# An FFN unit list in block order with a table of cluster limits, in a fused attention and maxout-FFN kernel

## The chip, the cores and the metric

The kernel runs on one NeuronCore of a Trainium2 chip. The metric is the device time of one execution in microseconds, lower being better. A core has five engines that run beside each other and wait for each other by semaphores: TensorE (PE; its weight loads are listed apart as PEld), VectorE (DVE), ScalarE (ACT), GpSimd (POOL) and SyncE (SP, which here only issues DMAs). Matmul results go to PSUM, which this kernel uses as eight banks of 128 x 512 fp32.

## What is computed

Attention over B = 8 batches, H = 8 heads, S = 576 tokens and D = 64, with 16 extra "beacon" keys and values that every query sees, and then a maxout FFN on all 4608 tokens:

```python
k_all = np.concatenate([beacon_k, k], axis=2)
v_all = np.concatenate([beacon_v, v], axis=2)
scores = scale * np.matmul(q, k_all.transpose(0, 1, 3, 2))
scores = np.where(causal, -1000000000.0, scores)
a = softmax(scores)
x = np.matmul(a, v_all).transpose(0, 2, 1, 3).reshape(B * S, H * D)
h = np.maximum(np.maximum(x @ w1, x @ w2), x @ w3)      # 512 -> 768
out = h @ w_out                                         # 768 -> 512
```

## The kernel before

**Attention in pairs.** Two heads make a pair p, four pairs (pi = 0 to 3) a batch b, and there are 32 pairs. From pair 8 on each pair is one turn of the loop at line 1027. `emit_burst` (line 526) issues its scores as 12 small matmuls (L517) into all eight PSUM banks, and ScalarE takes the exponentials (L534) four times, a pair of banks each. `emit_masks` (L556) has GpSimd clear what lies behind the diagonal. At an even p, `emit_pv_whole` (line 614) multiplies the two pairs before it with the values (L634, 108 and more matmuls into four banks), and ScalarE copies the result out (L644, L645) and makes the reciprocal of the sums (L650 to L652). What remains, the product of both, is `finish` (L657): two VectorE multiplies of 128 x 576, one for each 128 rows of `xT`, the FFN's transposed input. `finish` is issued only after the FFN units of that turn. At pi = 0 it writes the last values of the batch before, and so raises `ready`.

**FFN in units.** The 4608 tokens are nine blocks tb of 512. A block has 18 mm1 units (three weight matrices times six slices of 128 hidden features; four matmuls L709 that accumulate over the four row groups ct of `xT`, and one VectorE operation that starts the maximum (L726) or joins it (L728) in the tile `hT`) and four mm2 units (128 tokens each; six matmuls L756 with `hT` as weights, one VectorE copy L763 into a tile `y`, and a store on SP, L788). Block 0 counts twelve half units and six whole ones in place of the 18. So there are 22 units a block (UPB) and 198 in all. Blocks of 512 tokens do not fall together with batches of 576: nearly all blocks need the last values of a batch. Each unit carries in `need` the value of `ready` from which it may be issued.

**The order of the work** is written out by hand and nothing reorders it. The list `units` (lines 793 to 811) gives the sequence of the units. In it, a block tb from 1 on begins with its own first two mm1 units, then come the four mm2 units of block tb - 1, then its other 16 mm1 units. (Block 0's mm2 units stand behind its own mm1 units.) In each turn of the pair loop the cluster of units that follows the scores goes on until `allowed` (lines 1033 to 1037), which grows evenly by 22 units for four pairs, or until a unit's `need` is not met. The last unit of a cluster is issued with `close`, which cuts it into two halves of 256 columns (`parts`, L717), so that the last PSUM eviction before the next burst is short. Inside the cluster, the transposes of the next pair come after the first unit (only for p + 1 < 16), and `plan`'s entries for (p, 0) after the second: casts on GpSimd (L267, L310), loads (L229, L294), stores of cast pairs to DRAM (L379) and their transposing fetches (L386, L387) on SP. `store_y` issues a store of every `y` that was complete before the present unit.

PSUM banks are handed out in turn (`next_bank`, L156); a burst takes the pairs of banks that have been free longest (`next_pairs`, L161).

After the last pair (lines 1059 to 1068), three units are issued, then the last `emit_pv_whole`, then two units, then `finish`, and then all units that are left.

Of the kernel before, what the change touches and what calls it, by code (L numbers as in the profile page):

```python
# [16 lines left out]
def kernel(  # L17
# [23 lines left out]
    TOKB = 512  # L41
# [18 lines left out]
    PPB = H // 2  # L60
# [23 lines left out]
    FIRST_BURST = 2 * PPB  # L84
# [350 lines left out]
    def place_beacons(p, copy):  # L435
        b, pi = divmod(p, PPB)
        copy(kTs[p % NT][:, 0:Nb], bT[:, pi, Nb * b : Nb * (b + 1)])
# [54 lines left out]
    def emit_scores(p, gi):  # L492
        if gi == 0:
            at[p] = at_pool.tile([128, AT_W], BF16, name="at_sb")
        kT = kTs[p % NT]
        qT = qTs[p % NT]
        ps = sc_psum.tile()
        off = 0
        for t, q0, q1 in groups(p)[gi]:
            for e in range(2):  # L500
                hs = slice(64 * e, 64 * e + 64)
                nc.tensor.matmul(  # L502
                    ps[:, e, off : off + q1 - q0],
                    kT[hs, 128 * t : 128 * t + 128],
                    qT[hs, q0:q1],
                    start=True,
                    stop=True,
                    tile_position=(64 * e, 0),
                )
            off += q1 - q0  # L510
        nc.scalar.activation(  # L511
            out=both_heads(p, gi), in_=ps[:, :, 0 : g_width(p, gi)], func=AF.Exp, scale=scale
        )
# [29 lines left out]
    def emit_masks(p, gi, dve=False):  # L543
        masked.add((p, gi))
        off = 0
        for t, q0, q1 in groups(p)[gi]:
            n = rows_of(p, t, q1)
            lo, hi = max(q0, k_tok[t]), min(q1, k_tok[t] + n)
            if lo < hi:
                view = both_heads(p, gi)[0:n, :, off + lo - q0 : off + hi - q0]  # L550
                x0 = lo - k_tok[t]
                if dve:
                    m = tri[0:n, None, x0 : x0 + hi - lo]
                    nc.vector.tensor_mul(view, view, m.to_broadcast([n, 2, hi - lo]))
                else:
                    nc.gpsimd.affine_select(  # L556
                        out=view,
                        in_=view,
                        compare_op=ALU.is_ge,
                        fill=0.0,  # L560
                        base=x0,
                        pattern=[[0, 2], [1, hi - lo]],
                        channel_multiplier=-1,
                    )
            off += q1 - q0
# [225 lines left out]


    units = []
    outputs = []
    for tb in range(n_tokb):
        need = 2 * ((TOKB * (tb + 1) - 1) // S) + 1
        blocks = []
        if tb == 0:
            for n, lo in ((0, 0), (need, MID)):
                for i in range(2):  # L800
                    for ft in range(0, n_ft, 2):
                        units.append((n, mm1_halves, (tb, ft, i, lo, lo + MID)))
        for i in range(2 if tb == 0 else 0, 3):
            for ft in range(n_ft):
                blocks.append((need, mm1_unit, (tb, ft, i)))
        units += blocks[:2] + outputs + blocks[2:]
        outputs = [(need, mm2_unit, (tb, tt)) for tt in range(TOKB // 128)]
        if tb == 0:
            units += outputs
            outputs = []  # L810
    units += outputs
    END = len(units)
    UPB = END // n_tokb
    done = [0]
# [48 lines left out]
    def start():  # L863
        keep_busy(12)
        load_half(0, 0, nc.sync)
        load_half(0, 1, nc.scalar)
        load_half(1, 0, nc.sync)
        load_beacons(0, 1, bk32_0, nc.scalar)
        load_half(1, 1, nc.scalar)
        make_identity(nc, ident)  # L870
        nc.gpsimd.memset(tri, 1.0)
        nc.gpsimd.affine_select(
            out=tri,
            in_=tri,
            compare_op=ALU.is_ge,
            fill=0.0,
            base=0,
            pattern=[[1, 128]],
            channel_multiplier=-1,
        )  # L880
        load_quad(1, 0)
        load_quad(0, 1)
        load_quad(1, 1)
        next_load(3)
        cast_half(0, 0, by_dve)
        cast_half(0, 1, by_act)
        by_dve(bk16_0, bk32_0)
        turn_half(0, 0, False, by_act)
        keep_busy(3)
        turn_beacons(0, 1, bk16_0)  # L890
        cast_half(1, 0, by_dve)
        cast_half(1, 1, by_dve)
        keep_busy(2)
        turn_half(1, 0, True)
        place_beacons(1, by_dve)
# [6 lines left out]
    def steps(p):  # L902
        return [[0, 1], [2, 3]]
# [55 lines left out]
    for b in range(2, B):  # L959
        p = b * PPB  # L960
# [5 lines left out]
    for b in range(B_PE, B):  # L966
        p = b * PPB
# [7 lines left out]
    N_FIRST = 11  # L975

    def emit_all():
        start()
        for group, fns in first_steps:
            if group:  # L980
                emit_scores(*group)
            for fn in fns:
                fn()
        first = done[0]
        n_step = 0
        n_y = 0
        for p in range(PPB, FIRST_BURST):
            for s, gs in enumerate(steps(p)):
                for gi in gs:
                    emit_scores(p, gi)  # L990
                for gi in gs:
                    emit_masks(p, gi)
                for args in pv_at.pop((p, s), ()):
                    emit_pv(*args)
                    invert_sums()

                n_step += 1
                allowed = first + n_step * (UPB - first) / N_FIRST
                if s == 0:
                    if p == PPB + 2:  # L1000
                        emit_ffn(allowed)
                    turn_pair(p + 1, by_act, "pv" if p < PPB + 2 else "sc")
                    if p != PPB + 2:
                        emit_ffn(allowed)
                    place_beacons(p + 1, by_act)
                    store_y(n_y)
                    n_y = len(y_out)
                    for fn in plan.pop((p, s), ()):
                        fn()
                    emit_ffn(allowed)  # L1010
                    n_y = len(y_out)
                    emit_ffn(allowed)
                    multiply()
                else:
                    emit_ffn(allowed)
                    multiply()
                    store_y(n_y)
                    n_y = len(y_out)
                    for fn in plan.pop((p, s), ()):
                        fn()  # L1020
                    emit_ffn(allowed)
                    n_y = len(y_out)
                while emit_ffn(allowed):
                    pass
        v_tiles.pop(0)

        for p in range(FIRST_BURST, NPAIR):
            b, pi = divmod(p, PPB)
            emit_burst(p)
            finish = emit_pv_whole(p // 2 - 1) if p % 2 == 0 else None  # L1030
            for gi in range(NG):
                emit_masks(p, gi)
            n_step += 2
            if n_step <= N_FIRST:
                allowed = first + n_step * (UPB - first) / N_FIRST
            else:
                allowed = UPB + (n_step - N_FIRST) * UPB / (2 * PPB)
            n = 0
            while may_emit(allowed):
                n_y = len(y_out)  # L1040
                emit_ffn(allowed, next_psum, not may_emit(allowed, 1))
                store_y(n_y)
                n += 1
                if n == 1 and p + 1 < B_PE * PPB:
                    turn_pair(p + 1, by_act, "any")
                    place_beacons(p + 1, by_act)
                if n == 2:
                    for fn in plan.pop((p, 0), ()):
                        fn()
            assert n >= 2  # L1050
            if finish:
                finish()
            for s in range(2):
                for fn in plan.pop((p, s), ()):
                    fn()
            if pi == 0:
                v_tiles.pop(b - 1)
        assert not plan and not loads and not pv_at
        for _ in range(3):
            emit_ffn(END, next_psum)  # L1060
        finish = emit_pv_whole(NPAIR // 2 - 1)
        for _ in range(2):
            emit_ffn(END, next_psum)
        finish()
        store_y(len(y_out))
        while emit_ffn(END - 1, next_psum):
            store_y(len(y_out))
        mm2_last(n_tokb - 1, TOKB // 128 - 1, (0, 320, 512))
# [33 lines left out]
```

## Time and profile before

| | us |
|---|---|
| median of three runs | 300.87 (299.56 to 300.94) |
| the profiled execution | 301.9 |
| its span, first to last instruction | 300.2 |
| PE busy | 282.3 (94%) |
| DVE, ACT, POOL busy | 180.9, 148.0, 132.7 |
| mean granted TensorE clock | 0.983 |

A profile is of one execution. Its page gives each engine's busy time, the span in 40 slices of 7.5 us, the chain of waits that ended last, and groups of instructions by source line; line numbers such as L709 are those of the kernel before. In a timeline, a row has the start in us, the time from the start of its first instruction to the end of its last, the engine, the line, the operation, the count, and in brackets the engine's idle time before it with what ended it. Matmuls overlap each other in the pipeline, so the distance between their starts, not their own duration, says how fast they go.

### The profile page before, as it was taken

What the parts mean: (1) busy time and instruction counts of PE and PEld (TensorE: products, weight loads), DVE (VectorE), ACT (ScalarE), POOL (GpSimd) and SP (SyncE); (2) the same over time, 40 slices, a digit from 0 to 9 for tenths busy, and PEclk for the clock granted to TensorE, in tenths of its full rate; (3) what the DMA queues carried; (4) which work ended last, traced back from release to release, by engine and by line L of the source; (5) the groups of instructions that cost most, each with busy time, mean ns of one, the idle gap of its engine ahead of it and who ended that gap; (6) DMA issues with size and microseconds to landing.
All of it is one profiled execution on the core that took longest, in us unless ns stands there. A gap on an engine that the chain in (4) does not pass through costs nothing.

```text
span 300.2 us, 8579 instructions
## 1 busy us (share of the span) xinstructions
PE 282.3 (94%) x3511; PEld 163.2 (54%) x3539; DVE 180.9 (60%) x330; ACT 148.0 (49%) x247; POOL 132.7 (44%) x253
## 2 busy tenths in 40 slices
PE   7789997999999999999999999999999998999994
PEld 3545664465656465546555787465546453444442
DVE  3743763537585649473847384738473856776772
ACT  3664485796667484747474747474746430000000
POOL 6170667476566864566456635663262300000000
PEclk9966999999999999999999999999999999999999
DMA  8978999999999999799979996997303000202103
GB/s 149 199 126 197 232 203 271 260 198 285 270 216 249 171 306 229 164 175 289 290 154 181 276 265 161 196 257 130 82 11 131 2 2 35 105 3 84 56 0 142
DMA packets 85319, 50.66 MB, mean 169 GB/s; under 512 B 64416, under 2 KB 80032, under 8 KB 85280
## 3 DMA queue, kind: packets, MB, share of 16 engines
q1 hardware_dynamic: 80672, 45.76, 66.0%
q0 software_dynamic: 4048, 4.03, 8.2%
q8 instruction: 27, 0.44, 0.7%
q10 hardware_dynamic: 560, 0.33, 0.5%
q14 instruction: 12, 0.10, 0.1%
HBM read 35.13 MB, written 14.22 MB: 164 GB/s over the span
## 4 chain that ended last, share of the span: by engine, by line
PE 78%; DMA 9%; DVE 5%; issue 2%; POOL 2%; SPq 1%; ACT 1%; POOLq 0%
PE acc L709 41%; PE acc L756 15%; PE acc L634 10%; DMA st<-in_v_dram 8%; PE acc L517 6%; DVE xT L657 3%; PE acc L600 2%; DVE hT L728 2%; PE acc L394 2%; ACT at_sb L511 1%; PE acc L502 1%; DMA h<-in_q_dram 1%; SPq L229 1%; POOL v_sb L310 1%; PE acc L737 1%
## 5 line engine op out<-in xcount | busy, mean ns | idle before, releaser
L709 PE MATMUL acc<-xT,w_sb 128*128 128x512 bf16 (+1 forms) x709 | 135.5, 340 | 4.5 <-DVE xT L657 3.3
L534 ACT ACTIVATE at_sb<-acc 128x416 bf16<-128x416 f32 (+1 forms) x96 | 75.3, 868 | 69.3 <-PE acc L517 58.5
L709 PEld LDWEIGHTS <-w_sb 128*128 128x128 bf16 x732 | 69.1, 98 | 59.8 <-issue 4.4
L556 POOL TENSOR_SCALAR_AFFINE_SELECT at_sb<-at_sb 128x256 bf16<-128x256 bf16 (+2 forms) x148 | 58.7, 411 | 89.9 <-ACT at_sb L534 71.6
L728 DVE TENSOR_TENSOR hT<-hT,acc 128x512 bf16<-128x512 bf16 (+1 forms) x119 | 69.8, 610 | 37.3 <-PE acc L709 34.7
L726 DVE CAST hT<-acc 128x512 bf16<-128x512 f32 (+1 forms) x49 | 33.1, 680 | 31.0 <-PE acc L709 23.0
L756 PE MATMUL acc<-w_out_sb,hT 128*128 128x512 bf16 (+1 forms) x241 | 46.8, 347 | 0.2
L267 POOL CAST p<-st 96x768 bf16<-96x768 f32 x56 | 44.5, 825 | 0.0
L763 DVE COPY y<-acc 128x512 f32<-128x512 f32 (+1 forms) x41 | 24.7, 613 | 18.8 <-PE acc L756 17.7
L756 PEld LDWEIGHTS <-hT 128*128 128x128 bf16 x246 | 23.9, 98 | 21.8 <-DVE hT L728 0.2
L511 ACT ACTIVATE at_sb<-acc 128x992 bf16<-128x992 f32 (+6 forms) x32 | 26.3, 863 | 14.3 <-PE acc L502 14.3
L517 PE MATMUL acc<-qT,kT 64*128 64x80 bf16 (+4 forms) x288 | 24.7, 280 | 0.6 <-ACT at_sb L511 0.6
L781 ACT COPY y<-acc 128x320 f32<-128x320 f32 x1 | 0.4, 427 | 48.0 <-PE acc L774 48.0
L634 PE MATMUL acc<-at_sb,v_sb 128*32 128x80 bf16 (+5 forms) x936 | 23.2, 243 | 0.0
L657 DVE TENSOR_TENSOR xT<-raw,recip 128x576 bf16<-128x576 f32 x26 | 20.7, 839 | 0.0
L517 PEld LDWEIGHTS <-kT 64*128 64x128 bf16 x288 | 12.4, 94 | 15.0 <-issue 10.7
L310 POOL CAST v_sb<-st 128x1536 bf16<-128x1536 f32 (+2 forms) x21 | 18.4, 896 | 1.5 <-DMA st<-in_v_dram 1.5
L634 PEld LDWEIGHTS <-v_sb 128*32 128x32 bf16 (+1 forms) x936 | 15.6, 97 | 4.1
L644 ACT COPY raw<-acc 128x496 f32<-128x496 f32 x26 | 14.1, 611 | 5.8 <-PE acc L634 5.8
L634 PE MATMUL acc<-at_sb,ones 128*32 128x80 bf16 (+5 forms) x468 | 14.0, 245 | 0.0
L737 PE MATMUL acc<-xT,w_sb 128*128 128x256 bf16 x96 | 13.0, 285 | 0.6 <-DVE qT L430 0.6
L502 PE MATMUL acc<-qT,kT 64*128 64x288 bf16 (+7 forms) x112 | 11.1, 287 | 2.2 <-ACT at_sb L511 2.2
(65 smaller groups left out, 172.6 us busy)
## 6 DMA issues: line engine op xcount, KB each, us to landing
out_dram<-y SPq DMA_DIRECT2D x35, 256.0 KB, 3.8
st<-in_q_dram SPq DMA_DIRECT2D x28, 288.0 KB, 5.2
st<-in_k_dram SPq DMA_DIRECT2D x28, 288.0 KB, 6.3
st<-in_v_dram SPq DMA_DIRECT2D x24, 256.0 KB, 6.0
w_sb<-in_moe_w_dram POOLq DMA_DIRECT2D x6, 384.0 KB, 6.8
q_dram<-p SPq DMA_DIRECT2D x16, 144.0 KB, 3.1
k_dram<-p SPq DMA_DIRECT2D x16, 144.0 KB, 3.1
st<-in_v_dram SPq DMA_DIRECT2D x8, 224.0 KB, 5.4
```

The costliest lines, as they stand in the source:

```text
L267: cast(t16.rearrange("p r h d -> p h r d"), st[0:QP, i * NQ2 : (i + 1) * NQ2].rearrange("p (h r d) -> p h r d", h=2, r=QR),)
L511: nc.scalar.activation(out=both_heads(p, gi), in_=ps[:, :, 0 : g_width(p, gi)], func=AF.Exp, scale=scale)
L517: nc.tensor.matmul(ps, kTs[p % NT][hs, 128 * t : 128 * t + 128], qTs[p % NT][hs, q0:q1], start=True, stop=True, tile_position=(64 * e, 0),)
L534: nc.scalar.activation(out=both_heads(p, gi), in_=acc[:, first : first + 2, 0 : g_width(p, gi)], func=AF.Exp, scale=scale,)
L556: nc.gpsimd.affine_select(out=view, in_=view, compare_op=ALU.is_ge, fill=0.0, base=x0, pattern=[[0, 2], [1, hi - lo]], channel_multiplier=-1,)
L634: nc.tensor.matmul(acc[32 * j : 32 * j + 32, bank, lo + q0 - qa : lo + qb - qa], lhsT, at_view(PPQ * quad + j // 2, t, j % 2, q0, qb), sta ...
L657: nc.vector.tensor_mul(xT[:, 2 * g + i, c0 : c0 + S], raw[:, i], recip)
L709: nc.tensor.matmul(ps[:, a:b], w_in[i][:, ct, 128 * ft : 128 * (ft + 1)], xT[:, ct, x0 : x0 + b - a], start=(ct == 0), stop=(ct == n_ct - 1),)
L726: by_dve(h[:, lo:hi], ps[:, lo:hi])
L728: nc.vector.tensor_max(h[:, lo:hi], h[:, lo:hi], ps[:, lo:hi])
L756: nc.tensor.matmul(ps[:, lo:hi], hT[:, ft, 128 * tt : 128 * (tt + 1)], w_out_sb[:, ft, lo:hi], start=(ft == 0), stop=(ft == n_ft - 1),)
L763: nc.vector.tensor_copy(y[:, lo:hi], ps[:, lo:hi])
```

## The change

The list of units is written in plain block order: each block's four mm2 units stand directly behind its own 18 mm1 units. In the pair loop from p = 8 on, the even growth of `allowed` gives way to 20 for p = 8, and else to (b - 1) * 22 plus a number from a table by the pair's place in its batch: -4, 2, 7, 13. The code before pair 8 and after pair 31 is the same.

```diff
     units = []
-    outputs = []
     for tb in range(n_tokb):
         need = 2 * ((TOKB * (tb + 1) - 1) // S) + 1
-        blocks = []
         if tb == 0:
             for n, lo in ((0, 0), (need, MID)):
                 for i in range(2):
@@ -802,13 +800,9 @@
                         units.append((n, mm1_halves, (tb, ft, i, lo, lo + MID)))
         for i in range(2 if tb == 0 else 0, 3):
             for ft in range(n_ft):
-                blocks.append((need, mm1_unit, (tb, ft, i)))
-        units += blocks[:2] + outputs + blocks[2:]
-        outputs = [(need, mm2_unit, (tb, tt)) for tt in range(TOKB // 128)]
-        if tb == 0:
-            units += outputs
-            outputs = []
-    units += outputs
+                units.append((need, mm1_unit, (tb, ft, i)))
+        for tt in range(TOKB // 128):
+            units.append((need, mm2_unit, (tb, tt)))
     END = len(units)
...
             for gi in range(NG):
                 emit_masks(p, gi)
-            n_step += 2
-            if n_step <= N_FIRST:
-                allowed = first + n_step * (UPB - first) / N_FIRST
-            else:
-                allowed = UPB + (n_step - N_FIRST) * UPB / (2 * PPB)
+            allowed = 20 if p == FIRST_BURST else (b - 1) * UPB + (-4, 2, 7, 13)[pi]
             n = 0
```

## Prediction

> **What bounds the kernel now.** First the page's busy times.
>
> ```profile
> PE 282.3 (94%) x3511; PEld 163.2 (54%) x3539; DVE 180.9 (60%) x330; ACT 148.0 (49%) x247; POOL 132.7 (44%) x253
> ```
>
> PE is busy 94% of the span. Asked by stretch, the profile gives PE 177.33 of 181 us between 60 and 241 us, and 53.53 of 59.2 us behind that, both at a granted clock of 1.00. So PE sets the end, and what counts is where it stands still. The view of PE's waits is headed by
>
> ```profile
> PE acc L709 <- DVE xT L657: 3.3, 7, 1.0
> PE acc L502 <- ACT at_sb L511: 2.2, 5, 0.8
> ```
>
> The first row is the only wait that recurs in the second half: seven times mm1 waited for the multiplies that write a batch's last values. The second belongs to the time before 60 us, which the change leaves alone. The timeline round one of the seven, pair 17:
>
> ```profile
> 126.41 2.14 DVE L728 TENSOR_TENSOR hT<-hT,acc 128x512 bf16<-128x512 bf16 x4 [0.24 <-PE acc L709]
> ...
> 127.97 1.00 PE L517 MATMUL acc<-qT,kT 64*128 64x208 bf16 x12
> ...
> 128.47 1.63 DVE L657 TENSOR_TENSOR xT<-raw,recip 128x576 bf16<-128x576 f32 x2
> ...
> 128.93 0.81 PE L709 MATMUL acc<-xT,w_sb 128*128 128x512 bf16 x3
> ...
> 130.15 1.24 PE L709 MATMUL acc<-xT,w_sb 128*128 128x512 bf16 x5 [0.41 <-DVE xT L657]
> ```
>
> The reader is to see the order: the turn before ends with its maxima, the multiplies come behind them on DVE, PE does the burst of scores (L517), starts the next block's first mm1, gets through row groups 0 to 2, and stands before the fourth until DVE has done the second multiply. The outputs (L756), which need none of this, come after it, from 131.23.
>
> **What a stop costs.** The bracket counts from the modelled end of a pipelined matmul, so I use starts. The pitch comes from the tail, weight loads alone:
>
> ```profile
> 276.71 13.70 PEld L709 LDWEIGHTS <-w_sb 128*128 128x128 bf16 x64
> 290.53 0.96 PEld L756 LDWEIGHTS <-hT 128*128 128x128 bf16 x5
> 291.68 2.61 PEld L756 LDWEIGHTS <-hT 128*128 128x128 bf16 x13 [0.20 <-DVE hT L728]
> ```
>
> Less one load of 0.10 us, 13.60 / 63 = 0.216 us for a 512-column matmul. At pair 17 the fourth was due at 128.93 + 3 x 0.216 = 129.58 and started at 130.15: 0.57 us lost. In the same way pair 13 lost 0.60 (97.77, then 99.02), pair 25 0.57 (189.32, 190.54) and pair 29 0.57 (219.50, 220.72). Pair 21 has 256-column matmuls at half the pitch, and the eighth waited: 159.11 + 7 x 0.109 = 159.87, started at 160.33, 0.46 lost. Sum of the five: 2.77 us. The other two waits are in the tail:
>
> ```profile
> 245.93 2.33 PE L709 MATMUL acc<-xT,w_sb 128*128 128x512 bf16 x9
> ...
> 247.87 0.69 DVE L728 TENSOR_TENSOR hT<-hT,acc 128x512 bf16<-128x512 bf16 x1 [0.17 <-PE acc L709]
> 248.48 1.42 DVE L657 TENSOR_TENSOR xT<-raw,recip 128x576 bf16<-128x576 f32 x2
> 249.28 0.38 PE L709 MATMUL acc<-xT,w_sb 128*128 128x512 bf16 x1 [1.02 <-DVE xT L657]
> ...
> 249.95 1.24 PE L709 MATMUL acc<-xT,w_sb 128*128 128x512 bf16 x5 [0.29 <-DVE xT L657]
> ```
>
> Two units of four matmuls and the first two of block 7 take ten places from 245.93, so the eleventh was due at 248.09 and came at 249.28: 1.19 lost; the next was due at 249.50 and came at 249.95: 0.45. Tail: 1.64. **Together 4.41 us.**
>
> **The change part by part.**
>
> *Order.* By the table, units 35 to 39 end block 1 in pair 12's cluster (before too: unit 40 wasn't ready), and the same holds each 22 units later. Pair 13's cluster (and 17, 21, 25, 29) keeps six units, but mm2 x 4, then mm1 x 2. The tail likewise: units 148 and 149 end block 6, then come its four outputs, then block 7. So the mm1 that needs the new values starts 24 x 0.216 = 5.2 us later in its cluster, and the stops it had were 0.6 and 1.64 us: all seven go, with over 3 us to spare. **-4.41.**
>
> *What is late next.* The outputs read `hT`, whose last maxima precede the multiplies on DVE. At pair 17 they end at 126.41 + 2.14 = 128.55, before the first output could start (128.93): nothing. In the tail the last maximum ends at 248.56, and only the sixth weight load of the first output, due at 247.66 + 5 x 0.216 = 248.74, needs it. The same succession stands in the tail shown: five loads, a sixth at 291.68 where 290.53 + 1.08 = 291.61 was due, 0.07 lost. It will occur in two more places: +0 to 0.14, I take **0.05**. The outputs' copies queue behind the multiplies, which end at 130.10, as the first output does (128.93 + 1.30): no wait, and further banks follow in turn.
>
> *Table.* One unit moves from each batch's pair pi = 2 to pi = 3 (clusters 5, 6, 5, 6 for 6, 5 and so on). PE's sum is unchanged. The pair after a five-unit cluster with a value product is seen at pair 16: ACT's last reciprocal ends at 126.30, the next burst starts at 127.97. So ACT is ready, and GpSimd's masks follow the burst as they did.
>
> *Closing.* Six-unit clusters now all end with a halved mm1 instead of, half the time, a halved mm2. In the instruction lists PE has 14 matmuls and 14 loads fewer. Two of 256 columns cost 2 x 0.109 against 0.216: 14 x 0.002 = **-0.03**. The burst behind finds its last banks a little later: bursts last 0.94 (120.33 to 121.27) or 0.96 (127.97 to 128.93) behind five units, 0.97 behind a halved mm2 and 1.01 (205.45 to 206.46) behind six ended by a maximum. At most two longer bursts a batch by 0.04 to 0.08, one shorter by 0.05: about 0.04 a batch, **+0.2** (0 to 0.4).
>
> *SP.* The store of a batch's first output now stands ahead of two v loads, two fetches and a pair's store. It must wait for its copy, at pair 13 until about 97.77 + 1.30 + 0.24 + 0.69 = 100.0:
>
> ```profile
> 92.66 5.52 SPq L294 DMA_DIRECT2D st<-in_v_dram  x3
> 98.29 2.46 SPq L386 DMA_TRANSPOSE qT<-q_dram  x1
> ```
>
> The v loads that went out by 98.2 slip to 100, the fetch by 3 to 4 us. Fetches land in 2.5 to 6.2 us, and this one is used by pair 16's burst at 120.33; the v cast is at 135. At the later batches SP gets to this place after the copy is done (pair 17: 132.18, copy at 131.0). Cost **0**; without that cover it would be up to 4 us at one batch.
>
> Sum: -4.41 + 0.05 - 0.03 + 0.2 = **-4.2 us**. The profiled execution's own 301.9 becomes 297.7. The median shown is 1.03 below that execution, which gives **296.7 us**, a gain of 1.4%.
>
> **A rule against the sum.** All of this takes 0.216 us as PE's own rate. The row above has it over 63 matmuls, with DVE's maxima waiting 0.17 us for PE each time (the bracket at 247.87 is such a one), so nothing downstream holds PE. The Trainium skill, "TensorE: Matmul & The Clock Gate", section "Back-to-back issue gap", says that a stream of loads and matmuls runs at about 131 ns for 512 columns, and that 216 is the isolated gap; by it PE would have slack in every cluster, and a removed stop would be worth nothing. The trace disagrees, and the measurement decides; it is the smaller part of rival 1 below, 0.02 of its chance.
>
> **Rivals.**
> 1. *The stop is only moved* (PE paced by another engine, or the outputs stand behind the multiplies' queue on DVE). Then the five clusters give nothing and the tail its 1.6: 300.87 - 1.6 = 299.3; nothing at all gives 300.9. Against it: DVE is idle 37.3 us before L728 alone, waiting for PE. 0.10.
> 2. *Slower: the granted clock drops under a closer stream.* Place: 60 to 300 us. Price: 240 us x 1% = 2.4 us for each hundredth of the clock, so it decides from 1.7 hundredths on; three hundredths give 300.87 - 4.2 + 7.2 = 303.9. Against it: from 256.2 to 290 us PE ran 33.64 of 33.80 us at a granted 1.00. 0.05.
> 3. *It doesn't do what it says:* excluded for the order by the instruction lists (L756 directly behind the burst in all five places).
>
> **How the numbers follow.** Forecast 0.85, rival 1 0.10, rival 2 0.05. Half a per cent, 1.5 us, is about what a measurement of this kernel can tell from no change. The forecast's own bounds: all stops recovered and bursts no longer, 296.4; the higher ends of the burst, `hT` and SP terms (0.4, 0.14, 1 of the 4 us leaking through), 298.0; the three runs shown spread by 1.4, so a median can lie 0.7 to either side, and the runs' clock and DMA phases add some. 295.3 to 298.8 holds the forecast and leaves out both rivals, 0.15 together.
>
> **What would show it.** Right: "PE acc L709 <- DVE xT L657" gone from PE's waits; L756 behind L517 at pairs 13, 17, 21, 25, 29 without a gap; first L709 of block 7 near 250 (252.8 without the five earlier stops, less 2.7), not waiting; PE idle about 4 us less; span near 296.0. Wrong: a new PE wait on DVE before L756 or L517 of over 0.2 us, on a DMA before a burst, or a granted clock under 0.97.

## The result and the profile after

The changed kernel took 296.69 us (median of four runs, 295.47 to 301.74) against 300.9 us (299.56 to 303.11) for the kernel before: a ratio of 0.9859 with a 95% interval of 0.9812 to 0.9906. A second set of runs gave 0.9855 (0.9783 to 0.9927). The forecast was 296.7 us, so 0.986.

The run of 301.74 us counts as a slow one and is left out of the ratio; since the first profile was taken of it, the lines below are from the profile of a repeat, whose execution took 299.8 us with a span of 298.1 us.

Whole executions of this kernel differ by some 5 us, and the traces show where: in the time before pair 8's burst, in which both programs are the same. I therefore compare the stretch **from the start of pair 8's burst** (the first L517 in the timeline) **to the end of the span**, called "the stretch" from here on. Its first rows, for the kernel before and then the repeat:

```profile
59.83 0.26 PE L517 MATMUL acc<-qT,kT 64*128 64x208 bf16 x2
```

```profile
61.72 0.26 PE L517 MATMUL acc<-qT,kT 64*128 64x208 bf16 x2
```

In the kernel before the stretch is 300.19 - 59.83 = 240.36 us. In the changed kernel it is 236.40 us in the first profile (300.02 - 63.62) and 236.37 us in the repeat (298.09 - 61.72). So it repeats to 0.03 us, and the change is worth 3.96 to 3.99 us of it. The kernel before was profiled once, but a kernel below that shares its loop (tail_only) takes 175.79 us from pair 8's burst to pair 31's, where the kernel before takes 175.80.

Busy times by stretch, for the kernel before and then the repeat; the columns are the stretch, its length, busy time and count of PE, PEld, DVE, ACT and POOL, the granted clock, the DMA share and GB/s:

```profile
59.80:300.20 240.40, 231.06 (x2721) 131.29 (x2746) 149.20 (x240) 112.79 (x190) 100.86 (x188) 1.00 0.69 160
```

```profile
61.70:298.10 236.40, 231.72 (x2733) 129.83 (x2732) 148.64 (x240) 112.77 (x190) 100.47 (x188) 1.00 0.70 163
```

The reader is to see that the length falls by 4.0 us while every engine's busy time stays within 1.5 us of what it was and the clock stays at 1.00. PE was idle for 9.3 us of this time and is idle for 4.7 us now (6.0 in the first profile; the counts differ because some matmul records are missing from a trace, so idle time is the rougher measure). Hardly any work was saved; a wait was.

The head of PE's waits in the repeat:

```profile
PE acc L502 <- ACT at_sb L511: 2.4, 6, 0.8
PE acc L470 <- DVE busy L186: 1.3, 1, 1.3
```

The row with L709 and L657 has gone; both rows shown belong to the time before pair 8. PE's timeline at pair 17, where eight matmuls of a new block (two mm1 units) stood ahead of the outputs in the kernel before:

```profile
129.51 1.00 PE L517 MATMUL acc<-qT,kT 64*128 64x208 bf16 x12
130.47 5.34 PE L756 MATMUL acc<-w_out_sb,hT 128*128 128x512 bf16 x24
135.64 1.57 PE L709 MATMUL acc<-xT,w_sb 128*128 128x512 bf16 x9
```

The 24 output matmuls follow the scores without a bracket, and 24 x 0.216 = 5.18 us later, at 135.64, the next block's mm1 starts. The tail, from the timeline of all engines:

```profile
247.22 4.05 PE L756 MATMUL acc<-w_out_sb,hT 128*128 128x512 bf16 x18
247.42 0.69 DVE L728 TENSOR_TENSOR hT<-hT,acc 128x512 bf16<-128x512 bf16 x1 [0.17 <-PE acc L709]
248.02 1.42 DVE L657 TENSOR_TENSOR xT<-raw,recip 128x576 bf16<-128x576 f32 x2
```

The multiplies run from 248.02 to 249.44 as late after block 6's last maximum as they did. What has changed is that PE has outputs to do meanwhile.

### The profile page after: what moved, and what is told of

Read it like the earlier page. It is cut to its first block, busy times and chain, and to the rows that moved or that the text cites. A ratio compares the mean times of both kernels' runs of the same rounds, so it can differ in the third digit from the quotient of the medians.

```text
span 300.0 us, 8555 instructions
## 1 busy us (share of the span) xinstructions
PE 288.2 (96%) x3497; PEld 165.5 (55%) x3525; DVE 180.9 (60%) x330; ACT 148.0 (49%) x247; POOL 132.4 (44%) x253
## 3 DMA queue, kind: packets, MB, share of 16 engines
q0 software_dynamic: 4048, 4.03, 8.3%
## 4 chain that ended last, share of the span: by engine, by line
PE 89%; DMA 4%; ACT 2%; issue 1%; SPq 1%; POOL 1%; DVE 0%; POOLq 0%
PE acc L709 43%; PE acc L756 15%; PE acc L634 10%; PE acc L517 8%; DMA st<-in_v_dram 4%; PE acc L600 3%; PE acc L502 2%; ACT at_sb L511 2%; PE acc L394 2%; PE acc L417 2%; PE acc L470 2%; PE acc L737 1%; PE acc L403 1%; SPq L229 1%; POOL v_sb L310 0%
## 5 line engine op out<-in xcount | busy, mean ns | idle before, releaser
L709 PE MATMUL acc<-xT,w_sb 128*128 128x512 bf16 (+1 forms) x727 | 134.7, 336 | 1.2 <-issue 0.2
L709 PEld LDWEIGHTS <-w_sb 128*128 128x128 bf16 x748 | 71.4, 98 | 56.7 <-issue 0.6
L728 DVE TENSOR_TENSOR hT<-hT,acc 128x512 bf16<-128x512 bf16 (+1 forms) x119 | 70.2, 610 | 38.2 <-PE acc L709 35.5
L756 PE MATMUL acc<-w_out_sb,hT 128*128 128x512 bf16 (+1 forms) x209 | 46.8, 373 | 0.3
L756 PEld LDWEIGHTS <-hT 128*128 128x128 bf16 x216 | 20.5, 98 | 22.7 <-DVE hT L728 0.6
L517 PE MATMUL acc<-qT,kT 64*128 64x80 bf16 (+4 forms) x288 | 25.2, 280 | 0.6 <-ACT at_sb L511 0.6
L517 PEld LDWEIGHTS <-kT 64*128 64x128 bf16 x288 | 12.4, 94 | 15.5 <-issue 11.8
L657 DVE TENSOR_TENSOR xT<-raw,recip 128x576 bf16<-128x576 f32 x26 | 20.7, 839 | 0.0
L502 PE MATMUL acc<-qT,kT 64*128 64x288 bf16 (+7 forms) x112 | 12.6, 323 | 2.4 <-ACT at_sb L511 2.4
L737 PE MATMUL acc<-xT,w_sb 128*128 128x256 bf16 x96 | 13.7, 295 | 0.6 <-DVE qT L430 0.6
```

The costliest lines, as they stand in the source:

```text
L517: nc.tensor.matmul(ps, kTs[p % NT][hs, 128 * t : 128 * t + 128], qTs[p % NT][hs, q0:q1], start=True, stop=True, tile_position=(64 * e, 0),)
L657: nc.vector.tensor_mul(xT[:, 2 * g + i, c0 : c0 + S], raw[:, i], recip)
L709: nc.tensor.matmul(ps[:, a:b], w_in[i][:, ct, 128 * ft : 128 * (ft + 1)], xT[:, ct, x0 : x0 + b - a], start=(ct == 0), stop=(ct == n_ct - 1),)
L728: nc.vector.tensor_max(h[:, lo:hi], h[:, lo:hi], ps[:, lo:hi])
L756: nc.tensor.matmul(ps[:, lo:hi], hT[:, ft, 128 * tt : 128 * (tt + 1)], w_out_sb[:, ft, lo:hi], start=(ft == 0), stop=(ft == n_ft - 1),)
```

## Experiments

What each measured:

| kernel | stretch, us | against before | time against before (95%) |
|---|---|---|---|
| before | 240.36 | | |
| changed, repeated | 236.37 | -3.99 | 0.9855 (0.9783 to 0.9927) |
| order_only | 237.87 | -2.49 | 0.9854 (0.9789 to 0.9919) |
| order_only_whole | 236.78 | -3.58 | one run, no interval |
| table_only | 240.50 | +0.14 | 1.0039 (0.9988 to 1.0089) |
| tail_old | 237.99 | -2.37 | 0.9884 (0.9838 to 0.9929) |
| tail_only | 238.70 | -1.66 | 0.9993 (0.9936 to 1.0049) |
| one_first | 236.45 | -3.91 | 0.9885 (0.9822 to 0.9949) |
| one_first_tail | 236.13 | -4.23 | 0.9854 (0.9814 to 0.9894) |
| no_close | 240.75 | +0.39 | 1.0022 (0.9982 to 1.0063) |

The intervals are 0.8 to 1.4% wide, so the times confirm the larger gains only: that of tail_only, 1.66 us or 0.55%, lies inside its interval together with no gain at all. The stretch, at a granted clock of 1.00 in every profile, tells the parts apart.

**The changed kernel again.** No edit.

> The changed kernel again, for more runs and another profile. Theory (the seven stops of PE before the next block's mm1 are gone, worth 4.4 us, less 0.2 for longer bursts): 1.3 to 1.5% under the kernel before; in the profile no wait of L709 on the multiplies L657, and from the start of pair 8's burst to the end of the span about 236.4 us, where the kernel before has 240.4 (300.2 - 59.8). Rival (the difference comes from the first 60 us, which vary with the loads): that stretch within 0.5 us of 240.4, and the gain in the time before pair 8.

236.37 us, no wait of L709 on L657: the theory's number. The rival falls: the stretch is 4 us shorter than before, and the time before pair 8 was 1.9 us longer here than in the profile of before.

**The table without the order.** Old list of units, with

```diff
+            allowed = 20 if p == FIRST_BURST else (b - 1) * UPB + (-4, 2, 7, 13)[pi]
```

in place of the even growth.

> The table of limits with the old unit list: one unit moves from each batch's pair pi = 2 to pi = 3, nothing else. Theory (the table moves no stop): seven waits of L709 on L657 as before, 240.2 to 240.7 us from pair 8's burst to the end, time within 0.3% of before. Rival (evener clusters gain by themselves): 239 us or less.

```profile
PE acc L709 <- DVE xT L657: 3.3, 7, 1.0
```

The row of before stands again to the digit, and the stretch is 240.50 us. The table alone gains nothing.

**The order without the table.** Block order, with the even growth put back.

> The unit list in block order, with the even growth of the limits kept instead of the table. Pair 12's cluster (and 16, 20, 24, 28) now takes the first output as a sixth unit and halves it; the three other outputs open the next cluster. Theory (order alone gains): three outputs are 3.9 us ahead of the mm1, more than the 0.6 us needed, so all stops are gone: 236.1 to 236.8 us from pair 8's burst to the end, time 1.3 to 1.5% under before. Rival (the table is needed): the output at a cluster's end waits for the maximum just before it, its copies push the multiplies back, and the stops return: 237.5 us or more.

237.87 us is outside the theory's 236.1 to 236.8: by the number the rival's 237.5 is passed, but the rival's account of it is only half right. The second row of PE's waits:

```profile
PE acc L756 <- DVE hT L728: 1.4, 5, 0.3
```

No stop on the multiplies came back. Instead there is a new one, in the five clusters whose last unit is now an output. The timeline before pair 17 in this kernel:

```profile
131.82 0.64 PEld L756 LDWEIGHTS <-hT 128*128 128x128 bf16 x5
...
132.29 0.69 DVE L728 TENSOR_TENSOR hT<-hT,acc 128x512 bf16<-128x512 bf16 x1 [0.23 <-PE acc L709]
133.03 0.66 PEld L756 LDWEIGHTS <-hT 128*128 128x128 bf16 x7 [0.57 <-DVE hT L728]
```

Five weight loads pass, and the sixth, which needs the slice that L728 is still writing until 132.98, waits. My theory had missed that the last unit of a cluster is halved: its matmuls pass at 0.109 us, so the sixth load is due after 0.55 us, by the pitch, and not after 1.08. That was tried next. By starts each stop costs about 0.56 us (the fifth load starts at 131.82 + 0.64 - 0.10 = 132.36, the sixth was due at 132.47 and came at 133.03), 2.75 us for the five. Part of this comes back: the 23 bursts from pair 9 on sum to 21.91 us here and to 22.75 in the changed kernel, and the time from the first L774 to the end is 5.2 us instead of 5.5. Why the end is shorter here is open.

**The same with that output whole.** The halving is left out where the last unit is an output:

```diff
-    emit_ffn(allowed, next_psum, not may_emit(allowed, 1))
+    emit_ffn(allowed, next_psum, not may_emit(allowed, 1) and units[done[0]][1] is mm1_unit)
```

> order_only, but the last unit of a cluster is left whole where it is an output. Theory (the halved output stood 0.45 us before its sixth weights because five half matmuls pass in 0.55 us while the maximum ahead of it takes 0.9 us to come out): whole matmuls pass in 1.08 us, the wait of L756 on L728 falls from 1.4 us to under 0.4, while the whole copy costs the burst behind it about 0.18 us each: 236.6 to 237.4 us from pair 8's burst to the end. Rival (any output that stands directly behind the last maximum waits for it): the wait stays at 1.4 us, 238.5 us or more.

```profile
125.91 0.96 PEld L756 LDWEIGHTS <-hT 128*128 128x128 bf16 x5
127.12 0.10 PEld L756 LDWEIGHTS <-hT 128*128 128x128 bf16 x1 [0.25 <-DVE hT L728]
```

At the same place the sixth load comes 1.21 us after the first, 0.13 late by the pitch, and the row of L756 on L728 is gone from PE's waits. 236.78 us in a single profile, inside the theory's range; bursts behind a whole output take 1.15 to 1.24 us here. The table's share of the gain, 237.87 - 236.37 = 1.5 us, is thus to keep a halved output away from the maximum that it reads; it isn't needed for the stops on the multiplies.

**The loop without the tail.** The changed kernel, with the units from 150 on in the old order.

> The changed kernel, but from unit 150 on, the units behind the pair loop, in the old order: two mm1 units of block 7, the four outputs of block 6, and so on. Theory (five stops of 0.46 to 0.60 us in the loop, two of together 1.64 us in the tail): the two tail stops return and nothing else, 238.0 us from pair 8's burst to the end, 1.6 us over the changed kernel. Rival (the loop holds the whole gain): 236.4 us. Rival (the tail holds it): 240 us.

```profile
PE acc L709 <- DVE xT L657: 1.3, 2, 1.0
```

237.99 us, with the two tail waits of 1.0 and 0.3 back and none in the loop.

**The tail without the loop.** The mirror image: the kernel before, with block order from unit 150 on.

> The kernel before, with block order only from unit 150 on, the units behind the pair loop. Theory: the five stops of the loop stay, the two of the tail go: 238.8 us from pair 8's burst to the end, 1.6 us under the 240.4 of before. Rival (the loop holds the whole gain): 240.4 us.

```profile
PE acc L709 <- DVE xT L657: 1.9, 5, 0.4
```

238.70 us: five waits of the loop left, the tail's gone. The two halves, 2.37 and 1.66 us, add up to 4.03 us against 3.99 for both, so the two parts simply add.

**One output ahead instead of four.** With the table:

```diff
-        units += blocks[:2] + outputs + blocks[2:]
+        units += outputs[:1] + blocks[:2] + outputs[1:] + blocks[2:]
```

> The table, and a list in which one output of the block before, not four, stands ahead of a block's first two mm1 units; the other three follow these two. Theory (an output is 1.30 us of cover, the loop's stops need up to 0.60 us, the tail's 1.64): no stop in the loop, 0.3 to 0.4 us left in the tail, 236.7 us from pair 8's burst to the end. Rival (what counts is that the multiplies and the outputs' copies have the whole of the four outputs, 5.2 us, to get through VectorE): stops of 0.3 us or more in the loop as well, 238 us or more.

236.45 us, and in PE's timeline of the tail one stop is left, now at the fourth row group only:

```profile
246.21 0.81 PE L709 MATMUL acc<-xT,w_sb 128*128 128x512 bf16 x3
247.19 1.24 PE L709 MATMUL acc<-xT,w_sb 128*128 128x512 bf16 x5 [0.17 <-DVE xT L657]
```

Due at 246.21 + 0.65 = 246.86, it came at 247.19: 0.33 us, where 1.64 - 1.30 = 0.34 was left uncovered. In the loop there is no stop. So it is the amount of other work ahead that counts, and four outputs are more than the loop needs.

**One output ahead in the loop, four in the tail.** What the runs before pointed to.

> One output ahead of a block's first two mm1 units in the loop, as in one_first, and from unit 150 on the block order of the changed kernel. Theory (in the loop one output covers the stop and the cluster's halved last unit is an output, behind which bursts were shorter; in the tail four outputs are needed): 172.4 us from pair 8's burst to pair 31's, as in one_first, and 63.7 us from there to the end, as in the changed kernel: 236.1 us, 0.3 us under the changed kernel, which the times themselves cannot show. Rival (the 0.3 us of one_first was chance): 236.4 us.

172.41 us from pair 8's burst to pair 31's and 63.72 us from there to the end, 236.13 together: both parts came out as expected. It is 0.24 us shorter than the changed kernel; in the times (0.9854) that can't be seen.

**No halving.** The changed kernel, with every last unit of a cluster whole:

```diff
-    emit_ffn(allowed, next_psum, not may_emit(allowed, 1))
+    emit_ffn(allowed, next_psum)
```

> The changed kernel without halving the last unit of a cluster. Theory (a burst waits for the last evictions of the cluster before it, so their length is on PE's path): the last eviction takes 0.69 us instead of 0.42, bursts are 0.1 to 0.3 us longer at 24 places, 238.8 to 243 us from pair 8's burst to the end. Rival (the burst's own 1 us covers the eviction, and halving only adds matmuls): 236.0 to 236.5 us.

```profile
127.49 0.67 PE L517 MATMUL acc<-qT,kT 64*128 64x208 bf16 x6
128.40 0.39 PE L517 MATMUL acc<-qT,kT 64*128 64x336 bf16 x6 [0.23 <-DVE hT L728]
```

The burst breaks in two: its last matmuls wait for the bank that the whole eviction still holds. From pair 9 on bursts take 1.15 to 1.24 us here and 0.93 to 1.03 us in the changed kernel. The stretch is 240.75 us, 4.4 us longer. A missing halving alone would have eaten the whole gain.

## Why the prediction was right

**The stops.** Right in mechanism, place and size. The five of the loop were put at 2.77 us; the clusters of pairs 13, 17, 21, 25 and 29, from burst to next burst, became 0.59, 0.58, 0.47, 0.58 and 0.58 us shorter, 2.80 together. The tail was put at 1.64 us and gave 1.62: from the first L709 behind the last value product to the first L774 it is 48.69 us in the profile of before (245.93 to 294.62) and 47.07 in the first one of the changed kernel (247.41 to 294.48). Each half was also removed by itself (tail_old and tail_only).

**What is late next.** The weight loads do stand 0.08 us late in the two new places (248.16 where 247.00 + 1.08 = 248.08 was due), but the matmuls behind them don't: the 24 from 247.22 end where the next block's first L709 starts, at 252.40, which is 0.216 us each. Nothing of the 0.05 us was lost. What I had not priced is the same wait behind a halved output, since the table keeps that case from arising.

**The bursts: the right cause, too small.** I took +0.2 us with 0.4 as the upper end. The 23 bursts from pair 9 on sum to 22.23 us in the kernel before and to 22.75 in the changed one, **+0.5 us**, above my upper end. My own terms (two bursts longer by 0.04 to 0.08 us, one shorter by 0.05) allow 0.03 to 0.11 us a batch, and I took 0.04, near the low end, and let 0.4 us stand as a bound that they do not give. Behind the halved maximum of a six-unit cluster bursts take 1.02 to 1.03 us, and there are two such clusters a batch now: pair 18 went from 0.97 to 1.03, pair 20 from 0.94 to 1.02, and pair 19 from 1.01 to 0.96. That is 0.09 us a batch. one_first shows the same from the other side: with a halved output ahead of pair 18's burst it falls back to 0.97.

**The sum.** -2.80 - 1.62 + 0.5 - 0.03 = -3.95 us, with 0.03 for the time from the first L774 to the end (5.57 us before, 5.54 in the first profile of the changed kernel); measured -3.96 in the first profile and -3.99 in the repeat. The forecast was -4.2.

**The number.** That the median of 296.69 us meets the forecast of 296.7 to 0.01 us is luck. The four runs behind it lie 6.3 us apart, the six of the repeat have a median of 298.15, and the forecast gain was itself 0.2 us too large. The sign "span near 296.0" did not show in either profile (300.0 and 298.1 us), because both reached pair 8 later than the profile of before. What bears the prediction out is the stretch.

**SP.** The store of the first output did stand ahead of the loads and fetches and did wait. SP in the repeat, at pair 13:

```profile
102.04 0.36 SPq L788 DMA_DIRECT2D out_dram<-y  x1
102.50 1.14 SPq L294 DMA_DIRECT2D st<-in_v_dram  x2
103.74 1.21 SPq L386 DMA_TRANSPOSE qT<-q_dram  x1
```

The fetch is issued 4.95 us behind pair 13's burst (98.79), where it was 1.47 us (98.29 - 96.82) before: 3.5 us later, as reckoned. Pair 16's burst at 121.77 shows no idle time of PE before it. So the cover was there, and the cost was nothing.

**The rivals.** That the stop is only moved: refuted for the changed kernel, and seen in order_only, though behind the maximum and not behind the multiplies. (Of DVE's 37.3 us of idle time before L728, which I gave as waiting for PE, 34.7 us were that.) The slower clock: not seen, 1.00 over the whole stretch. PE with slack at a pitch of 0.216 us: each removed stop came off the time in full, which it would not have done with slack. This speaks against the Trainium skill's figure of 131 ns ("TensorE: Matmul & The Clock Gate", section "Back-to-back issue gap") here too.

## What to carry to other kernels

Where the bound engine stops at a fixed place in each round, look for work of its own that is already due and needs nothing of what it waits for, and put it exactly there; the price of the stop, taken from the distance between starts and not from the idle bracket, is then the gain, as long as that work is longer than the stop. Moving such work also moves who stands directly behind whom: check what the moved unit itself reads and in what shape it is issued (order_only lost 1.5 of its 4 us to that). When whole executions scatter by more than the effect, measure from a point where the programs begin to differ.

## What was not expected

**The beginning goes with the scatter.** All eleven profiles run the same program until pair 8, and its burst starts anywhere from 58.1 to 64.0 us. What differs before it is PE's rate. From 4 to 32 us the granted clock is 1.00 in three profiles (order_only_whole, no_close, one_first_tail), where pair 8 starts at 58.1 to 59.0 us. It is 0.82 in two (before and one_first, 59.8 and 59.7 us), 0.76 in tail_only (61.4), 0.70 in the repeat (61.7) and 0.57 in order_only (64.0): the lower the clock, the later the burst.

The other three (the first profile of the changed kernel, table_only and tail_old) are given a clock of 1.00 there too, and yet pair 8 starts at 62.6 to 63.6 us. Their matmuls contradict that clock. The first eight matmuls of L737, in one_first_tail and then in the first profile of the changed kernel:

```profile
22.84 1.03 PE L737 MATMUL acc<-xT,w_sb 128*128 128x256 bf16 x8 [0.22 <-DVE xT L680]
```

```profile
28.44 1.89 PE L737 MATMUL acc<-xT,w_sb 128*128 128x256 bf16 x8
```

In the kernel before, where the clock given at that place is 0.50, they take 1.89 us too. So a granted clock of 1.00 is worth checking against the time that equal matmuls take. The Trainium skill, "TensorE: Matmul & The Clock Gate", section "What's actually happening", describes a gate that opens after a busy window, whose phase differs from run to run, and puts its cost under 1% of a typical kernel. Here the three profiles at a full clock reach pair 8 at 58.5 us in the mean and the one at 0.57 at 64.0 us, 5.5 us later, over 1% of the kernel. That the gate is the cause, and not merely goes along with it, was not tried.
